# Two-layer expert network behind a channel attention: the first pair's v transposed on VectorE alone, with the opening rearranged around it

## The chip, the cores and the metric

The kernel runs on one core of one Trainium2 chip. The metric is the device time of one execution in microseconds (us); smaller is better. The engines are TensorE (PE for its matmuls, PEld for its weight loads), VectorE (DVE), ScalarE (ACT), GpSimd (POOL) and SyncE (SP), which here only issues DMAs.

## The reference

q, k and v are 6016 x 256, fp32. Channel attention, then two feed-forward layers:

```python
qn = q / (norm(q, axis=rows) + 1e-6); kn = k / (norm(k, axis=rows) + 1e-6)
s = kn.T @ qn / tau                    # 256 x 256
a = softmax(s, axis=-1)                # denominator + 1e-9
x = v @ a                              # 6016 x 256
h = x @ w_in;  x = (h * sigmoid(1.702 * h)) @ w_out        # 256 -> 2048 -> 256
h = x @ w2_in; out = maximum(0.01 * h, h) @ w2_out         # 256 -> 2048 -> 256
```

The weights come as 64-bit words and are turned into fp32 in the kernel.

## The kernel before, in words

**Numbers.** Most products are made of three fp32r matmuls over a high and a low half of each operand: (high, high), (low, high), (high, low), in the order that `terms` writes. `halves(hi, lo, raw)` makes the halves: a rounding copy on ScalarE gives the high half, and a subtraction on VectorE gives the low one.

**Stages.** First the kernel streams q and k and sums the 256 x 256 scores in two PSUM banks (y00 for half 0, y10 for half 1). The second half of the scores' last 16 rows is held back and handed to TensorE in portions, `second_half(count)`, so that it has work while the softmax is prepared. Instead of v @ a, the kernel folds a into the first layer's weights: `fold(f)` multiplies the softmax (halves `eth`, `etl`) with piece f of w_in (8 pieces, `wi`), scales it by the softmax's denominators (`fold_scale`) and makes the halves `wa[f]`. Piece 0 is folded in two halves by hand (kc = 0 after `softmax(0)`, kc = 1 after `softmax(1)`), as soon as each half of the softmax is there. Rows of v are handled in pairs of 512-column blocks (u = 0, 1), each in two halves of the channels (kc = 0, 1), with v turned so that channels lie on partitions: `xa[0]` holds kc = 0, `xbt` kc = 1. `first_products(kc, pairs)` are the first pair's products with piece 0, and `hidden_first(f)` is the rest of its hidden layer: activation (`act`), halves `gd`, later the products with w_out (`put`, `emit_y`).

**The first pair's v.** kc = 0 comes by eight DMAs of 64 KB each, in runs of 128 B (`blocks_in`/`blocks_of`: 32 x 32 blocks laid so that one VectorE transpose of 32 x 32 blocks, `turn_blocks(u)`, turns it). kc = 1 comes by one DMA of 512 KB in runs of 512 B, and TensorE turns it with eight 128 x 128 transposes (`transpose_v`) into the free PSUM banks y00 and y11. All of it lands in the place of the tenth q/k tile (`qk(V_TILE)`).

**The order.** Everything is written out by hand; each engine runs its instructions in the order of the program, and waits on semaphores. Weight pieces are turned into fp32 by a generator, `jobs()`, of which `go_on(n)` runs n steps. Each piece of w_in and w_out takes five steps on VectorE (`convert`): two or three integer operations (L211, L216, L220), then a copy for the high half and a subtraction for the low half. Numbering the steps from 1: wi0 is 1 to 5, wo0 6 to 10, wi1 11 to 15, wi2 16 to 20, wo1 21 to 25 (the subtraction is the last of each). Three pieces can be in flight. The third step of a piece frees its buffer, issues the next load (`next_load`) and calls `scale_next`, which has ScalarE scale the next landed piece (L181), unless `held` is set; `scale_next_piece` does so once by hand. `held` is set in the opening and cleared in `hidden_first(0)`:

```python
                    halves(gd[:, 0, u], gd[:, 1, u], h[:, u])
                    if f == 0 and u == 1:
                        held.clear()
                        scale_next()
                    go_on(1)
```

So the kernel before has run 12 steps when `hidden_first(0)` begins. In `hidden_first(0)` and `hidden_first(NF)` five more follow, then come `fold(1)`, which needs both halves of wi1 (step 15), two more, `hidden_first(1)` with `go_on(6)`, `fold(2)` and `go_on(2)`; the products of f = 1 with wo1 (step 25) follow.

Of the kernel before, what the change touches and what calls it, by code (L numbers as in the profile page):

```python
# [7 lines left out]
F32 = mybir.dt.float32  # L8
# [3 lines left out]
AF = mybir.ActivationFunctionType  # L12
# [5 lines left out]
def tile_kernel(  # L18
# [28 lines left out]
    nc = tc.nc  # L47
# [53 lines left out]
    def subtract(out, in0, in1):  # L101
        add(out, in0, in1, ALU.subtract)
# [11 lines left out]
    with tc.manual_schedule():  # L114
# [48 lines left out]
        def next_load():  # L163
            if to_load and len(raws) < 3:
                load_piece(to_load.pop(0))
# [21 lines left out]
        def scale_next_piece():  # L187
            held.clear()
            scale_next()
            held.append(True)  # L190
# [113 lines left out]
        def go_on(count):  # L304
            for _ in range(count):
                next(work, None)
# [25 lines left out]
        def qk(j):  # L332
            return big[(j // 2 + 2) % 4][:, j % 2]
# [18 lines left out]
        def blocks_of(x, p, u, kc, a):  # L352
            cols = slice(kc * P + a * SB, kc * P + (a + 1) * SB)
            s = start_of(p, u)
            return x[s:s + width[p], cols].rearrange("(b j) i -> j b i", j=SB)

        def blocks_in(t, p, a):
            return t[a * SB:(a + 1) * SB, :width[p]].rearrange("j (b i) -> j b i", i=SB)
# [57 lines left out]
        def second_half(count):  # L416
            for j, r in late_rows[:count]:
                scores(j, (1,), (r,))
            del late_rows[:count]
# [24 lines left out]
        for j in range(LATE + 1):  # L444
            t, n = qk(j), rows[j]
            scores(j, range(KC) if j < LATE else (0,))
            squares(j)
            if j + AHEAD <= last:
                load_qk(j + AHEAD)
            if j == V_TILE:  # L450
                next_load()
                nc.sync.dma_start(out=taub, in_=tau.partition_broadcast(P))
                vblocks = [qk(V_TILE)[:, 0, 2 * u:2 * u + 2, :].rearrange("p r c -> p (r c)") for u in range(2)]
                vrows = qk(V_TILE)[:, 1].rearrange("p r (s c) -> p (r s) c", c=P)
                for u in range(2):
                    for a in range(P // SB):
                        nc.sync.dma_start(
                            out=blocks_in(vblocks[u], 0, a), in_=blocks_of(v, 0, u, 0, a)
                        )
                nc.sync.dma_start(  # L460
                    out=vrows, in_=v[:2 * BLK, P:].rearrange("(t p) c -> p t c", p=P)
                )
                for _ in range(2):
                    next_load()

        for j in range(LATE + 1, last - 1):
            squares(j)
# [2 lines left out]
            scores(j, (0,))  # L470
        vt = {}

        def turn_blocks(u):
            vt[0, u] = front.tile([P, 2, C], F32, tag="sq", name="vt", bufs=6).rearrange("p r c -> p (r c)")
            nc.vector.transpose(out=vt[0, u], in_=vblocks[u])

        nc.vector.reciprocal(out=rtau, in_=taub)
        scale_next_piece()
        go_on(1)
        turn_blocks(0)  # L480
        second_half(1)
        norms()

# [14 lines left out]
        def spread():  # L498
            for kc in range(KC):
                nc.tensor.matmul(  # L500
                    nrm[:, C + kc * P:C + (kc + 1) * P],
                    lhsT=rn[:, kc:kc + 1].to_broadcast([P, P]), rhs=ident,
                    start=True, stop=True,
                )
            nc.scalar.copy(rq, nrm[:, C:2 * C])

        def transpose_v(tags):
            for u, tag in enumerate(tags):
                vt[1, u] = bank(tag)
                for i in range(BLK // P):  # L510
                    nc.tensor.transpose(  # L511
                        vt[1, u][:, i * P:(i + 1) * P], vrows[:, u * (BLK // P) + i], ident
                    )

        def split_v(kc, u):
            dst = xbt if kc else xa[0]
            halves(dst[:, 0, u], dst[:, 1, u], vt[kc, u])

        def softmax(h):

            nc.vector.tensor_tensor_reduce(
                out=sc[:, h], in0=s_ps[h][:, :C], in1=rq, scale=rk[:, h:h + 1],
                scalar=-3.0e38, op0=ALU.mult, op1=ALU.max, accum_out=mx[:, h:h + 1],
            )
            nc.vector.tensor_scalar(
                out=nmx[:, h:h + 1], in0=mx[:, h:h + 1], scalar1=-1.0, scalar2=None, op0=ALU.mult
            )
            nc.scalar.activation(
                out=ex[:, h], in_=sc[:, h], func=AF.Exp, bias=nmx[:, h:h + 1],
                scale=1.0, accum_out=den[:, h:h + 1],  # L530
            )

        def turn(h):
            for d in range(KC):
                nc.tensor.transpose(  # L535
                    et[:, h * C + d * P:h * C + (d + 1) * P], ex[:, h, d * P:(d + 1) * P], ident
                )

        def split_e(h):
            cols = slice(h * P, (h + 1) * P)  # L540
            src = et[:, h * C:(h + 1) * C].rearrange("p (d c) -> p d c", d=KC)
            nc.scalar.copy(eth[:, :, cols], src)
            subtract(etl[:, :, cols], src, eth[:, :, cols].bitcast(F32))
            nc.vector.tensor_scalar_add(rden[:, h:h + 1], den[:, h:h + 1], 1e-9)
            nc.vector.reciprocal(out=rden[:, h:h + 1], in_=rden[:, h:h + 1])
# [8 lines left out]
                    pw, lhsT=e[:, d, c0], rhs=wi[:, x, d], start=i == 0, stop=i == len(todo) - 1  # L554
                )

        def fold_scale(raw, pw, kc):
            nc.scalar.activation(
                out=raw[:, 0::3] if kc == 0 else raw[:, 1:3],
                in_=pw.rearrange("p (s n) -> p s n", s=2), func=AF.Copy,  # L560
                scale=rden[:, kc:kc + 1],
            )

        def fold_half(raw, f, kc):
            at = slice(0, 4, 3) if kc == 0 else slice(1, 3)
            hi, lo = wa[f][:, 0, at], wa[f][:, 1, at]
            (nc.vector.tensor_copy if kc else nc.scalar.copy)(hi, raw[:, at])
            subtract(lo, raw[:, at], hi.bitcast(F32))

        go_on(1)  # L570
        second_half(4)
        spread()
        nc.scalar.copy(xa[0][:, 0, 0], vt[0, 0])
        softmax(0)
        go_on(2)
        turn_blocks(1)
        go_on(1)
        second_half(5)
        et = bank("h3")
        turn(0)  # L580
        split_e(0)
        subtract(xa[0][:, 1, 0], vt[0, 0], xa[0][:, 0, 0].bitcast(F32))
        split_v(0, 1)
        scale_next_piece()
        go_on(1)
        second_half(2)
        wi0 = ready.pop(0)
        raw0 = early.tile([P, 4, P], F32, tag="tp", name="raw")
        pw = bank("y01")
        pw0 = [pw[:, kc * C:(kc + 1) * C] for kc in range(KC)]  # L590
        fold_products(pw0[0], wi0, 0)
        fold_scale(raw0, pw0[0], 0)
        fold_half(raw0, 0, 0)
        second_half(len(late_rows))
        transpose_v(("y00", "y11"))
        softmax(1)
        go_on(2)

        hp0 = {}

        def first_products(kc, pairs):
            for s, u in pairs:
                if kc == 0:
                    hp0[s, u] = bank(f"h{2 * s + u}")
                at = ((A11, A12), (A21, A22))[s][kc]
                x = xbt if kc else xa[0]
                terms(hp0[s, u], (wa[0][:, 0, at], wa[0][:, 1, at]), (x[:, 0, u], x[:, 1, u]),
                      kc == 0, kc == KC - 1)

        first_products(0, [(0, 0)])  # L610
        turn(1)
        split_e(1)
        scale_next_piece()
        go_on(1)
        split_v(1, 0)
        first_products(0, [(1, 0)])
        fold_products(pw0[1], wi0, 1)
        fold_scale(raw0, pw0[1], 1)
        fold_half(raw0, 0, 1)
        nc.sync.dma_start(out=w1raw[0], in_=raw0)  # L620
        split_v(1, 1)
        nc.scalar.preload_act_table(AF.Gelu_apprx_sigmoid)
        first_products(0, [(0, 1), (1, 1)])
        go_on(3)

        def fold(f):

# [412 lines left out]
```

## Time and profile before

| | |
|---|---|
| time, median of 3 runs | 1034.83 us (1034.72 to 1035.46) |
| the profiled execution's own time | 1034.38 us |
| its span, first to last instruction | 1032.6 us |
| TensorE matmuls busy | 1027.5 us (100%) |
| VectorE, ScalarE busy | 775.1 us (75%), 596.9 us (58%) |
| mean granted TensorE clock | 0.999 |

The span is what the trace covers; the execution's own time is 1.8 us longer. Matmuls are pipelined, and a matmul's recorded time includes the time in which it overlaps the next, so a row of n matmuls is best read by its start and the start of the row behind it. Times in the rows are us from the start of the span.

### The profile page before, as it was taken

The page shows a single profiled execution, that of the slowest core. Times are in us where ns is not written, and L with a number is a line of the kernel's source. Part 1 is how long each engine was busy: PE and PEld are TensorE (multiplying, and loading weights), DVE is VectorE, ACT ScalarE, POOL GpSimd, SP SyncE. Part 2 cuts the span into 40 slices and gives each one's busy share as a digit, 9 for nine tenths or more (in the row PEclk, how much of TensorE's full clock was granted, in tenths as well). Part 3 has the DMA queues.
Part 4 walks back from the last instruction along what each step waited for, and adds up shares of the span by engine and source line. Part 5 has one row for each costly group of instructions (what it writes and reads, how often), then busy time and mean ns, then how long its engine had stood idle before and what let it go on. Part 6 is the DMA issues. An engine that isn't in the chain of part 4 may idle for free.

```text
span 1032.6 us, 12743 instructions
## 1 busy us (share of the span) xinstructions
PE 1027.5 (100%) x4664; PEld 868.3 (84%) x4664; DVE 775.1 (75%) x1220; ACT 596.9 (58%) x906; POOL 0.8 (0%) x7
## 2 busy tenths in 40 slices
PE   9999999999999999999999999999999999999998
PEld 8888888888888888888998888888888888888997
DVE  7899868788888888887767666667577667667655
ACT  7675556566666666666555555555555555455453
POOL 0000000000000000000000000000000000000000
PEclk9999999999999999999999999999999999999999
DMA  9865323015115224214644003001100200300202
GB/s 352 249 163 153 126 49 92 11 31 165 60 52 168 77 65 126 80 56 150 239 150 144 1 1 72 11 1 31 52 0 16 67 1 1 77 1 1 42 1 36
DMA packets 124863, 81.84 MB, mean 79 GB/s; under 512 B 97664, under 2 KB 108928, under 8 KB 123520
## 3 DMA queue, kind: packets, MB, share of 16 engines
q1 hardware_dynamic: 120512, 80.04, 26.0%
q10 hardware_dynamic: 4288, 0.98, 0.5%
q8 instruction: 36, 0.59, 0.2%
q14 instruction: 27, 0.22, 0.1%
HBM read 55.05 MB, written 25.95 MB: 78 GB/s over the span
## 4 chain that ended last, share of the span: by engine, by line
PE 100%; DVE 0%; issue 0%
PE y L92 50%; PE h L92 44%; PE y L406 4%; PE h L553 1%; PE h L443 0%; PE y L553 0%; PE y L511 0%; PE h L426 0%; DVE o L706 0%; PE h L535 0%; PE h L500 0%
## 5 line engine op out<-in xcount | busy, mean ns | idle before, releaser
L92 PE MATMUL y<-gd,wo 128*128 128x512 f32 (+1 forms) x1248 | 296.2, 386 | 0.0
L92 PE MATMUL h<-xa,wa 128*128 128x512 f32 (+1 forms) x1152 | 276.1, 385 | 0.0
L92 PEld LDWEIGHTS y<-gd,wo 128*128 128x128 f32 x1248 | 233.9, 188 | 43.7
L92 PEld LDWEIGHTS h<-xa,wa 128*128 128x128 f32 x1152 | 216.0, 188 | 40.1
L92 PE MATMUL y<-g,wo 128*128 128x512 f32 (+1 forms) x1044 | 246.8, 385 | 0.0
L92 PEld LDWEIGHTS y<-g,wo 128*128 128x128 f32 x1044 | 196.0, 188 | 36.3
L92 PE MATMUL h<-xb,wa 128*128 128x512 f32 (+1 forms) x888 | 217.0, 385 | 0.0
L92 PEld LDWEIGHTS h<-xb,wa 128*128 128x128 f32 x888 | 166.6, 188 | 31.4 <-DVE wa L99 0.3
L99 DVE TENSOR_TENSOR tv<-tp,h 128x512 f32<-128x512 f32 (+1 forms) x88 | 59.2, 673 | 112.1 <-PE h L92 109.0
L99 DVE TENSOR_TENSOR cc<-tv,h 128x512 f32<-128x512 f32 (+1 forms) x176 | 115.8, 672 | 35.9 <-PE h L92 35.4
L96 DVE TENSOR_TENSOR gd<-cc,gd 128x1024 fp32r<-128x1024 f32 (+1 forms) x87 | 103.9, 1194 | 0.0
L877 ACT COPY tp<-h 128x512 f32<-128x512 f32 (+1 forms) x87 | 50.3, 578 | 91.3 <-PE h L92 90.7
L95 ACT CAST gd<-cc 128x1024 fp32r<-128x1024 f32 (+1 forms) x87 | 90.2, 1036 | 0.0
L650 ACT ACTIVATE cc<-cc 128x1024 f32<-128x1024 f32 (+2 forms) x49 | 50.3, 1027 | 39.1 <-DVE cc L99 39.1
L650 ACT ACTIVATE tt<-tt 128x512 f32<-128x512 f32 (+1 forms) x48 | 30.0, 625 | 72.3 <-DVE tt L99 72.3
L99 DVE TENSOR_TENSOR tt<-tv,h 128x512 f32<-128x512 f32 (+1 forms) x88 | 59.4, 675 | 9.6 <-PE h L92 0.5
L99 DVE TENSOR_TENSOR tt<-tt,h 128x512 f32<-128x512 f32 (+1 forms) x88 | 59.4, 675 | 9.5 <-DVE tt L99 0.5
L648 ACT ACTIVATE cc<-cc 128x1024 f32<-128x1024 f32 (+1 forms) x40 | 41.6, 1041 | 41.9 <-DVE cc L99 41.9
L99 DVE TENSOR_TENSOR g<-tt,g 128x512 fp32r<-128x512 f32 (+1 forms) x87 | 58.5, 673 | 7.2 <-ACT g L888 7.0
L648 ACT ACTIVATE tt<-tt 128x512 f32<-128x512 f32 (+1 forms) x40 | 24.9, 623 | 62.9 <-DVE tt L99 62.9
L99 DVE TENSOR_TENSOR g<-tp,g 128x512 fp32r<-128x512 f32 (+1 forms) x87 | 58.5, 673 | 0.1
L901 ACT CAST g<-tp 128x512 fp32r<-128x512 f32 (+1 forms) x87 | 53.2, 612 | 2.8
(110 smaller groups left out, 710.4 us busy)
## 6 DMA issues: line engine op xcount, KB each, us to landing
cv<-in_moe_w_in_dram SPq DMA_DIRECT2D x32, 256.0 KB, 3.4
cv<-in_moe_w_out_dram SPq DMA_DIRECT2D x16, 512.0 KB, 3.7
wa<-w2a SPq DMA_DIRECT2D x8, 896.0 KB, 5.6
x<-stg SPq DMA_DIRECT2D x5, 1024.0 KB, 4.2
stg<-x SPq DMA_DIRECT2D x5, 1024.0 KB, 5.2
out_dram<-o SPq DMA_DIRECT2D x80, 64.0 KB, 1.9
qk<-in_q_dram SPq DMA_DIRECT2D x8, 512.0 KB, 10.2
qk<-in_k_dram SPq DMA_DIRECT2D x8, 512.0 KB, 10.2
```

Of the source, the lines that this page charges most:

```text
L92: nc.tensor.matmul(dst, lhsT=w, rhs=x, start=start, stop=stop, skip_group_check=more)
L95: nc.scalar.copy(hi, raw)
L96: nc.vector.tensor_tensor(out=lo, in0=raw, in1=hi.bitcast(F32), op=ALU.subtract)
L99: nc.vector.tensor_tensor(out=out, in0=in0, in1=in1, op=op)
L406: nc.tensor.matmul(s_ps[h][:, :C], lhsT=t[:, 1, r, h * P:(h + 1) * P], rhs=t[:, 0, r, :], start=(j == 0 and r == 0), stop=(j == last and r ...
L553: nc.tensor.matmul(pw, lhsT=e[:, d, c0], rhs=wi[:, x, d], start=i == 0, stop=i == len(todo) - 1)
L648: nc.scalar.activation(out=out, in_=in_, func=AF.Gelu_apprx_sigmoid)
L650: nc.scalar.activation(out=out, in_=in_, func=AF.Prelu, alpha=0.01)
L877: nc.scalar.copy(tp, pa)
L901: nc.scalar.copy(g11[:, 0], tp)
```

## The change

The first pair's v is now loaded entirely as block loads: 16 DMAs of 64 KB instead of eight and one of 512 KB, with the weight pieces wo0 and wi1 issued after the second and the third group of four. VectorE turns all four blocks (`turn_blocks(kc, u)`), and TensorE's eight transposes go. The high and low halves of v are made by `v_high` (ScalarE) and `v_low` (VectorE) at places of their own. The second half of the softmax is rounded by VectorE instead of ScalarE. The second fold half's high part is written by ScalarE straight from PSUM, its low part is one VectorE operation from PSUM, and the raw half, which is only stored to DRAM, is written behind them. `first_products` takes the order (high, high), (low, high), (high, low) for kc = 0, and (high, high), (high, low), (low, high) for kc = 1. The load of ScalarE's Gelu table stands right behind the second Exp. The steps of `jobs()` are placed anew: 11 instead of 12 have run when `hidden_first(0)` begins, and step 8 stands behind the second fold half instead of in front of the first products.

```diff
-                vblocks = [qk(V_TILE)[:, 0, 2 * u:2 * u + 2, :].rearrange("p r c -> p (r c)") for u in range(2)]
-                vrows = qk(V_TILE)[:, 1].rearrange("p r (s c) -> p (r s) c", c=P)
-                for u in range(2):
+                vblocks = [
+                    qk(V_TILE)[:, i // 2, 2 * (i % 2):2 * (i % 2) + 2, :].rearrange("p r c -> p (r c)")
+                    for i in range(4)
+                ]
+                for i in range(4):
                     for a in range(P // SB):
                         nc.sync.dma_start(
-                            out=blocks_in(vblocks[u], 0, a), in_=blocks_of(v, 0, u, 0, a)
+                            out=blocks_in(vblocks[i], 0, a),
+                            in_=blocks_of(v, 0, i % 2, i // 2, a),
                         )
-                nc.sync.dma_start(
-                    out=vrows, in_=v[:2 * BLK, P:].rearrange("(t p) c -> p t c", p=P)
-                )
-                for _ in range(2):
-                    next_load()
+                    if i in (1, 2):
+                        next_load()
...
         scale_next_piece()
         go_on(1)
-        turn_blocks(0)
+        turn_blocks(0, 0)
+        go_on(1)
         second_half(1)
         norms()
...
-        def transpose_v(tags):
-            for u, tag in enumerate(tags):
-                vt[1, u] = bank(tag)
-                for i in range(BLK // P):
-                    nc.tensor.transpose(
-                        vt[1, u][:, i * P:(i + 1) * P], vrows[:, u * (BLK // P) + i], ident
-                    )
-
-        def split_v(kc, u):
+        def v_high(kc, u):
+            nc.scalar.copy((xbt if kc else xa[0])[:, 0, u], vt[kc, u])
+
+        def v_low(kc, u):
             dst = xbt if kc else xa[0]
-            halves(dst[:, 0, u], dst[:, 1, u], vt[kc, u])
+            subtract(dst[:, 1, u], vt[kc, u], dst[:, 0, u].bitcast(F32))
...
-            nc.scalar.copy(eth[:, :, cols], src)
+            (nc.vector.tensor_copy if h else nc.scalar.copy)(eth[:, :, cols], src)
...
-        def fold_half(raw, f, kc):
+        def fold_half(raw, f, pw, kc):
+
             at = slice(0, 4, 3) if kc == 0 else slice(1, 3)
             hi, lo = wa[f][:, 0, at], wa[f][:, 1, at]
-            (nc.vector.tensor_copy if kc else nc.scalar.copy)(hi, raw[:, at])
-            subtract(lo, raw[:, at], hi.bitcast(F32))
+            if kc == 0:
+                fold_scale(raw, pw, kc)
+                nc.scalar.copy(hi, raw[:, at])
+                subtract(lo, raw[:, at], hi.bitcast(F32))
+                return
+            fold_scale(wa[f][:, 0, :4], pw, kc)
+            nc.vector.scalar_tensor_tensor(
+                out=lo, in0=pw.rearrange("p (s n) -> p s n", s=2), scalar=rden[:, kc:kc + 1],
+                in1=hi.bitcast(F32), op0=ALU.mult, op1=ALU.subtract,
+            )
+            fold_scale(raw, pw, kc)
...
         go_on(1)
+        turn_blocks(0, 1)
         second_half(4)
         spread()
-        nc.scalar.copy(xa[0][:, 0, 0], vt[0, 0])
+        go_on(1)
         softmax(0)
-        go_on(2)
-        turn_blocks(1)
+        v_high(0, 0)
         go_on(1)
+        turn_blocks(1, 0)
+        v_low(0, 0)
         second_half(5)
         et = bank("h3")
         turn(0)
         split_e(0)
-        subtract(xa[0][:, 1, 0], vt[0, 0], xa[0][:, 0, 0].bitcast(F32))
-        split_v(0, 1)
+        v_high(0, 1)
+        v_low(0, 1)
         scale_next_piece()
         go_on(1)
+        turn_blocks(1, 1)
         second_half(2)
...
         fold_products(pw0[0], wi0, 0)
-        fold_scale(raw0, pw0[0], 0)
-        fold_half(raw0, 0, 0)
+        fold_half(raw0, 0, pw0[0], 0)
+        v_high(1, 0)
+        v_high(1, 1)
+        scale_next_piece()
         second_half(len(late_rows))
-        transpose_v(("y00", "y11"))
         softmax(1)
-        go_on(2)
...
-        first_products(0, [(0, 0)])
+        nc.scalar.preload_act_table(AF.Gelu_apprx_sigmoid)
+        v_low(1, 0)
+        go_on(1)
+        first_products(0, [(0, 0), (1, 0)])
         turn(1)
         split_e(1)
-        scale_next_piece()
-        go_on(1)
-        split_v(1, 0)
-        first_products(0, [(1, 0)])
+        v_low(1, 1)
+        first_products(0, [(0, 1)])
         fold_products(pw0[1], wi0, 1)
-        fold_scale(raw0, pw0[1], 1)
-        fold_half(raw0, 0, 1)
+        fold_half(raw0, 0, pw0[1], 1)
         nc.sync.dma_start(out=w1raw[0], in_=raw0)
-        split_v(1, 1)
-        nc.scalar.preload_act_table(AF.Gelu_apprx_sigmoid)
-        first_products(0, [(0, 1), (1, 1)])
-        go_on(3)
+        first_products(0, [(1, 1)])
+        go_on(4)
```

## Rows read from the trace of the kernel before

**Rows 1.** The page: busy us, share of the span and instructions of each engine

```profile
PE 1027.5 (100%) x4664; PEld 868.3 (84%) x4664; DVE 775.1 (75%) x1220; ACT 596.9 (58%) x906; POOL 0.8 (0%) x7
```

**Rows 2.** Timeline of TensorE's matmuls: start, us, instruction, out<-in, shape, count

```profile
48.28 1.04 PE L511 MATMUL y<-ident,qk 128*128 128x128 f32 x8
...
51.57 1.55 PE L92 MATMUL h<-xa,wa 128*128 128x512 f32 x6
52.96 3.04 PE L92 MATMUL h<-xb,wa 128*128 128x512 f32 x12
55.83 2.88 PE L92 MATMUL y<-gd,wo 128*128 128x512 f32 x12
58.55 0.64 PE L553 MATMUL h<-wi,eth 128*128 128x256 f32 x4
...
69.67 2.89 PE L92 MATMUL y<-gd,wo 128*128 128x512 f32 x12
```

**Rows 3.** Timeline of TensorE's weight loads; in brackets idle time and what ended it

```profile
49.85 0.20 PEld L535 LDWEIGHTS h<-ident,ex 128*128 128x128 f32 x2 [0.27 <-ACT ex L528]
```

**Rows 4.** Timeline of VectorE

```profile
47.86 0.42 DVE L99 TENSOR_TENSOR wa<-raw,wa 128x256 fp32r<-128x256 f32 x1
...
49.80 0.69 DVE L220 SCALAR_TENSOR_TENSOR ta<-cv,ta 128x512 int32<-128x512 int32 x1
...
57.58 0.69 DVE L99 TENSOR_TENSOR wi<-ta,wi 128x512 fp32r<-128x512 f32 x1
58.19 0.69 DVE L96 TENSOR_TENSOR gd<-h,gd 128x512 fp32r<-128x512 f32 x1
...
68.96 0.69 DVE L99 TENSOR_TENSOR wa<-raw,wa 128x512 fp32r<-128x512 f32 x1
```

**Rows 5.** Timeline of ScalarE

```profile
51.77 0.48 ACT L558 ACTIVATE raw<-y,rden 128x256 f32<-128x256 f32 x1
...
52.74 1.28 ACT L622 ACT_TABLE_LOAD   x1
...
56.92 0.57 ACT L648 ACTIVATE h<-h 128x512 f32<-128x512 f32 x1
57.53 0.62 ACT L95 CAST gd<-h 128x512 fp32r<-128x512 f32 x1
...
60.91 0.69 ACT L181 ACTIVATE cv<-cv 128x512 f32<-128x512 f32 x1
```

**Rows 6.** Timeline of SyncE: DMAs as they are issued

```profile
32.93 5.93 SPq L457 DMA_DIRECT2D qk<-in_v_dram  x8
...
39.44 0.58 SPq L157 DMA_DIRECT2D cv<-in_moe_w_out_dram  x1
...
50.56 0.37 SPq L157 DMA_DIRECT2D cv<-in_moe_w_out_dram  x1
...
61.45 2.09 SPq L725 DMA_DIRECT2D xr<-in_v_dram  x4
```

**Rows 7.** The page: DMA issues, count, KB each, median us to landing

```profile
cv<-in_moe_w_out_dram SPq DMA_DIRECT2D x16, 512.0 KB, 3.7
```

**Rows 8.** DMA issues of 61 to 82 us, columns as in the group above

```profile
xr<-in_v_dram SPq DMA_DIRECT2D x16, 64.0 KB, 2.6
```

**Rows 9.** VectorE's groups by shape, 28 to 140 us: busy us, mean ns | idle before

```profile
L475 DVE STREAM_TRANSPOSE vt<-qk 128x512 f32<-128x512 f32 x2 | 1.4, 708 | 0.0
...
L99 DVE TENSOR_TENSOR etl<-h,eth 128x256 fp32r<-128x256 f32 x2 | 0.8, 421 | 0.2 <-ACT eth L542 0.2
```

**Rows 10.** Busy time by stretch: engines (instructions), granted clock, DMA share, GB/s

```profile
4.00:6.00 2.00, 2.00 (x6) 1.55 (x6) 1.43 (x4) 1.26 (x5) 0.00 (x0) 1.00 0.91 272
...
37.00:38.00 1.00, 1.00 (x7) 0.87 (x6) 1.00 (x3) 0.00 (x0) 0.00 (x0) 1.00 0.64 94
...
41.00:42.00 1.00, 1.00 (x6) 0.87 (x6) 0.83 (x5) 1.00 (x1) 0.00 (x0) 1.00 1.05 312
...
1030.00:1033.00 3.00, 0.00 (x0) 0.00 (x0) 0.00 (x0) 0.00 (x0) 0.00 (x0) 0.56 0.43 70
```

More of the change, by code (lines that the diff above doesn't have):

```diff
@@ L471, in tile_kernel, with turn_blocks @@
         vt = {}
-        def turn_blocks(u):
-            vt[0, u] = front.tile([P, 2, C], F32, tag="sq", name="vt", bufs=6).rearrange("p r c -> p (r c)")
-            nc.vector.transpose(out=vt[0, u], in_=vblocks[u])
+        def turn_blocks(kc, u):
+            vt[kc, u] = front.tile([P, 2, C], F32, tag="sq", name="vt", bufs=6).rearrange("p r c -> p (r c)")
+            nc.vector.transpose(out=vt[kc, u], in_=vblocks[2 * kc + u])
         nc.vector.reciprocal(out=rtau, in_=taub)
@@ L555, in fold_products, with fold_scale @@
                 )
-        def fold_scale(raw, pw, kc):
+        def fold_scale(dst, pw, kc):
             nc.scalar.activation(
-                out=raw[:, 0::3] if kc == 0 else raw[:, 1:3],
+                out=dst[:, 0::3] if kc == 0 else dst[:, 1:3],
                 in_=pw.rearrange("p (s n) -> p s n", s=2), func=AF.Copy,
@@ L562, in fold_scale, with first_products @@
             )
-        def fold_half(raw, f, kc):
+        def fold_half(raw, f, pw, kc):
             at = slice(0, 4, 3) if kc == 0 else slice(1, 3)
             hi, lo = wa[f][:, 0, at], wa[f][:, 1, at]
-            (nc.vector.tensor_copy if kc else nc.scalar.copy)(hi, raw[:, at])
-            subtract(lo, raw[:, at], hi.bitcast(F32))
+            if kc == 0:
[9 more added lines that the diff above has]
+            fold_scale(raw, pw, kc)
+        def first_products(kc, pairs):
+            for s, u in pairs:
+                if kc == 0:
+                    hp0[s, u] = bank(f"h{2 * s + u}")
+                at = ((A11, A12), (A21, A22))[s][kc]
+                x = xbt if kc else xa[0]
+                wh, wl, ah, al = wa[0][:, 0, at], wa[0][:, 1, at], x[:, 0, u], x[:, 1, u]
+                order_of = ((wh, ah), (wh, al), (wl, ah)) if kc else ((wh, ah), (wl, ah), (wh, al))
+                for i, (w, a) in enumerate(order_of):
+                    nc.tensor.matmul(hp0[s, u], lhsT=w, rhs=a, start=kc == 0 and i == 0,
+                                     stop=kc == KC - 1 and i == 2)
+        hp0 = {}
         go_on(1)
+        turn_blocks(0, 1)
         second_half(4)
         spread()
-        nc.scalar.copy(xa[0][:, 0, 0], vt[0, 0])
+        go_on(1)
         softmax(0)
-        go_on(2)
-        turn_blocks(1)
+        v_high(0, 0)
         go_on(1)
+        turn_blocks(1, 0)
+        v_low(0, 0)
         second_half(5)
@@ L591, in tile_kernel @@
         fold_products(pw0[0], wi0, 0)
-        fold_scale(raw0, pw0[0], 0)
-        fold_half(raw0, 0, 0)
+        fold_half(raw0, 0, pw0[0], 0)
+        v_high(1, 0)
+        v_high(1, 1)
+        scale_next_piece()
         second_half(len(late_rows))
-        transpose_v(("y00", "y11"))
         softmax(1)
-        go_on(2)
[L599 to L608, printed above, removed]
-        first_products(0, [(0, 0)])
+        nc.scalar.preload_act_table(AF.Gelu_apprx_sigmoid)
+        v_low(1, 0)
+        go_on(1)
+        first_products(0, [(0, 0), (1, 0)])
         turn(1)
         split_e(1)
-        scale_next_piece()
-        go_on(1)
-        split_v(1, 0)
-        first_products(0, [(1, 0)])
+        v_low(1, 1)
+        first_products(0, [(0, 1)])
         fold_products(pw0[1], wi0, 1)
-        fold_scale(raw0, pw0[1], 1)
-        fold_half(raw0, 0, 1)
+        fold_half(raw0, 0, pw0[1], 1)
         nc.sync.dma_start(out=w1raw[0], in_=raw0)
-        split_v(1, 1)
-        nc.scalar.preload_act_table(AF.Gelu_apprx_sigmoid)
-        first_products(0, [(0, 1), (1, 1)])
-        go_on(3)
+        first_products(0, [(1, 1)])
+        go_on(4)
         def fold(f):
```

## The prediction, made blind

> **What bounds the kernel now.** I read the page first. TensorE's matmuls are busy 1027.5 us of a span of 1032.6, and no other engine is above 84% [rows 1]; the chain that ended last is TensorE's too. So a change counts only by the matmul time that it takes out and by the time for which it makes TensorE stand. Nothing behind the opening can give anything back, since TensorE has no idle time left there in which to catch up.
>
> Then the timeline of TensorE from 48 to 70 us. Read by starts, its matmuls of 512 columns follow each other every 0.23 us: six take 51.57 to 52.96, twelve 55.83 to 58.55 [rows 2]. In the opening the weight loads show small waits; the one that matters is 0.27 us for the second Exp, which frees `turn(1)` at 49.85 [rows 3]. All that the change can win lies there: the eight transposes (1.04 us in their row) and some tenths of waits, about 1.2 us in all. Measurement of this kernel tells about 0.2%, 2.07 us, from no change; a win of that size isn't in reach.
>
> Last, the timelines of VectorE, ScalarE and SyncE from 47 to 70 us, for what TensorE waits on next: VectorE has wi1's low half at 57.58 + 0.69 = 58.27 [rows 4], and TensorE first reads it with the third matmul of `fold(1)`, 58.55 + 2 x 0.12 = 58.78, where 0.12 is the pitch of a 256-column matmul (0.64 us for four with the overlap of the last) [rows 2]. That slack is 0.5 us.
>
> **The change part by part.**
>
> *The eight transposes go.* Without them TensorE runs the six matmuls of the first two products from 48.28 on, 6 x 0.23 = 1.4, to 49.66. `turn(1)` still waits for Exp until 49.85 [rows 3], so part of the gain turns into that wait. Behind `turn(1)` the order is as before with three matmuls fewer, so the products of xbt begin at 52.96 - 3 x 0.23 = 52.27: 0.69 us earlier.
>
> *Four VectorE turns instead of two, 2 x 0.71 us [rows 9].* The first extra one falls into time in which VectorE waits for the norms. The last one takes the place of a subtraction of nearly the same length, ahead of the first fold's low half, which so stays where it was: out at 47.86 + 0.42 = 48.28 [rows 4]. The second matmul, which now reads it, is due at 48.51. No cost, if the last block has landed when VectorE comes to it, 0.6 us (a turn's 0.71 less the overlap) before 47.86.
>
> *Sixteen block loads.* SyncE ends the first eight at 38.86. Then come wo0 (0.58), four blocks (2.09 for four in another stretch), wi1 (two issues like wo0, 1.2) and four blocks: 44.9 [rows 6]. The last issue begins near 44.4, and in that other stretch a block landed 2.6 us after its issue [rows 8]: 47.0, and VectorE comes to it at 47.26. While block loads moved, the DMA engines carried 94 GB/s at a busy share of 0.64; with longer runs it was 312 at 1.05 [rows 10]. By bandwidth, from 40.5 on (2.1 us behind the last of the first eight), wo0 and wi1 take 1.7 us each, and 256 KB of blocks 1.8 at the 147 GB/s of a full share: 47.5; 2.8 at 94 GB/s: 49.5. Bounds of the wait: nothing and 2.2 us. I take nothing, issue pace and landing of the same loads being the nearest rows.
>
> The Trainium skill, DMA: Bandwidth & Descriptors, "Why small descriptors are slow (HBM only)", says that each packet carries a fixed overhead, so that runs as short as these lose bandwidth. The trace agrees (94 against 312 GB/s); by the dearer of the two paces the last block comes 2.2 us late, and the forecast below would be 1039.2 instead of 1037.0.
>
> *Softmax rounding on VectorE.* At most 0.42 us, as a two-input operation of the same 256 columns from PSUM takes [rows 9]. It starts when `turn(1)` is through, near 50.35, and ends by 50.77; the fold that reads it comes at 50.83. No cost.
>
> *The second fold half from PSUM.* ScalarE's scaling can start at 51.77 as before, 0.48 us [rows 5], and now writes the high half itself: 52.25, where TensorE is ready for it at 52.27 (0.1 us to load the weights). The low half, one scalar-and-tensor operation of 256 columns from PSUM, isn't in the trace: between 0.42 [rows 9] and 0.69 (512 columns, L220 [rows 4]). I take 0.44, so 52.74. The third matmul wants it at 52.86. TensorE then ends the products of xbt at 55.20; before, it was 55.83. So far: -0.63 us.
>
> *The table load* (1.28 us [rows 5]) moves into ScalarE's idle time between 49.80 and 51.77. It costs nothing; in the old place it would now end at 54.02 again, and the first Gelu, which I expect at 53.3, would wait 0.7 us.
>
> *The steps of `jobs()`.* This is where I expect the loss. Before, step 8 ran at 49.80 and freed wo0's buffer, and SyncE issued wo1 at 50.56 [rows 4, 6]. Now step 8 stands behind the fold's low half: 52.74 + 0.61 = 53.35 (0.61 is VectorE's pitch, 57.58 to 58.19 [rows 4]). wo1 is issued at 53.42, and by the median of 3.7 us [rows 7] it lands at 57.15. And the count is one behind: step 13 was run before `held` was cleared in `hidden_first(0)`; now it comes after. Its `scale_next` therefore finds wi2 scaled and has ScalarE scale wo1 there, ahead of the third Gelu. Before, that scaling stood at 60.91, behind `fold(1)` [rows 5]. ScalarE would be free at 56.3 and waits for the landing until 57.2. Behind it queue: scaling 0.69, Gelu 0.57, rounding of gd 0.62 [rows 5]: 59.08. VectorE waits for that with gd's low half (0.69), and only then comes step 15, wi1's low half, since the count is one behind (before, it stood ahead of that gd: 57.58 and 58.19 [rows 4]): 59.12 + 0.61 + 0.69 = 60.41. TensorE ends its twelve y matmuls at 55.20 + 2.72 = 57.92, runs two matmuls of `fold(1)` and is due with the third at 58.15. It stands until 60.46: 2.31 us.
>
> *The step behind, once more.* Step 25, wo1's low half, ran in `hidden_first(1)` and now comes behind `fold(2)`'s last subtraction, which starts at 68.96 [rows 4]: in the old time scale it runs from 69.57 to 70.26. The second matmul of the row at 69.67 reads it, due at 69.90 [rows 2]; with the load of the weights it starts near 70.4. 0.5 us. Later pieces have slack, since each f runs 12 steps and needs 10.
>
> **Sum**, against the profiled execution's 1034.38 us: -0.63 + 2.31 + 0.5 = +2.18, so 1036.56. The median of the runs is 0.45 above that execution, so 1037.0 us: 0.21% slower. With the bounds of the single operations (0.25 for the low half, and estimates of 0.3 for wo1's landing and 0.3 for the last wait) this case spans 1036.3 to 1037.8.
>
> **The rivals.**
>
> *wo1 is there in time (not slower).* If it lands by 56.3, 2.9 us after its issue instead of 3.7, ScalarE doesn't wait, everything behind comes 0.95 us earlier, and the time is 1036.1, +0.12%. For it: TensorE and the DMA queue are otherwise quiet then. Against: the median over 16 such loads [rows 7]. It decides below 3.5 us, where the loss falls under 0.2%. If beside that VectorE's order hides step 15 altogether, only the -0.63 is left: 1034.2.
>
> *The last blocks come late.* Then the turn at 47.26, the fold's low half and the second softmax behind it slide, and step 8 with them: up to 2.2 us on the sum, 1037.2 to 1039.2, 1038 by the middle. It begins at a landing after 47.3, 0.3 later than I take it. For it: the bandwidth at 94 GB/s. Against: that stretch was not at full share.
>
> *The clock falls while TensorE stands.* With no matmul at the end of the kernel the mean granted clock of the last 3 us was 0.56 [rows 10]. In the first microseconds, where the clock column still prints 1.00, the pace was six matmuls in 2 us against seven in 1 us later, the low level of 1.2 GHz by its look [rows 10]. A stand of 2.3 us could bring that. Two to five us at half pace cost 1 to 2.5, less the 0.5 of the second wait, which VectorE would use to catch up: 1038.2. Against: no wait inside the kernel before has lowered it, but none was over 0.3 us.
> The Trainium skill, TensorE: Matmul & The Clock Gate, "HAM oscillation", has it that the clock goes back to half when TensorE idles between bursts; the end of this trace agrees, and no run here shows it for 2.3 us.
>
> *The change does what it says.* No new wait, 1.0 to 1.2 us won: 1033.7, still within 0.2%. Over 0.2% faster would need more matmul time than the change removes.
>
> **How the numbers follow.** The forecast 0.48, split at 1036.9 into 0.31 slower and 0.17 the same; wo1 in time or no wait 0.22, the same; late blocks 0.12 and the clock 0.15, slower; 0.03 for something that makes it faster by over 0.2%. So faster 0.03, same 0.39, slower 0.58. The range leaves out the cases with no new wait at all and the dearer part of late blocks and clock: 1034.6 to 1038.5 us.
>
> **What would show it.** The row of eight transposes is gone and products of xbt start near 52.3; a DMA wait on ScalarE at L181 near 57; TensorE standing some 2.3 us at the third matmul of `fold(1)`, released by VectorE's wi; a short wait at the y products behind `fold(2)`, released by wo. It is wrong if wi1's low half is out before 58.2, if the scaling of wo1 still stands behind `fold(1)`, or if VectorE waits for v's blocks near 47 us.

## The result, and the profile after

| | time, us | runs | TensorE's mean granted clock |
|---|---|---|---|
| before | 1034.78 (1033.90 to 1035.46) | 6 | 0.999 in the profile |
| after | 1040.96 (1038.98 to 1042.19) | 6 | 0.997 in four runs, 1.000 in two |

The ratio is 1.0059 [1.0046, 1.0072]: 6.2 us slower, outside the range of 1034.6 to 1038.5. The forecast had the sign and the largest of the new waits, and was 4 us short. The profiled execution took 1040.87 us, with a span of 1039.1; its clock was 0.997.

TensorE's timeline of the kernel after, around the opening (start, length, then engine, line, operation; in brackets the idle time before it and what ended it):

```profile
41.74 0.61 PE L501 MATMUL h<-ident,rn 128*128 128x128 f32 x4
...
50.32 1.41 PE L585 MATMUL h<-xa,wa 128*128 128x512 f32 x5 [1.60 <-DVE wa L99]
...
54.24 3.09 PE L585 MATMUL h<-xb,wa 128*128 128x512 f32 x12
57.16 2.88 PE L92 MATMUL y<-gd,wo 128*128 128x512 f32 x12
59.88 0.40 PE L549 MATMUL h<-wi,eth 128*128 128x256 f32 x2
62.62 0.51 PE L549 MATMUL h<-wi,eth 128*128 128x256 f32 x2 [2.34 <-DVE wi L99]
...
63.92 4.50 PE L92 MATMUL y<-gd,wo 128*128 128x512 f32 x12
...
75.84 2.83 PE L92 MATMUL y<-gd,wo 128*128 128x512 f32 x11 [0.26 <-DVE wo L99]
```

The row of eight transposes is gone. Against [rows 2] there are three new waits of over 0.2 us, at 50.32, 62.62 and 75.84. And at 63.92 twelve matmuls take 4.50 us, where the twelve at 57.16 take 2.72 by the next start (59.88).

The waits of TensorE's weight loads in the kernel after, 45 to 85 us (what waited and for what; us in total, times, longest):

```profile
PEld h L549 <- DVE wi L99: 2.5, 1, 2.5
PEld h L585 <- DVE wa L99: 2.0, 1, 2.0
PEld y L92 <- DVE wo L99: 0.7, 1, 0.7
...
```

VectorE's timeline of the same kernel:

```profile
44.58 0.71 DVE L475 STREAM_TRANSPOSE vt<-qk 128x512 f32<-128x512 f32 x1 [0.51 <-DMA qk<-in_v_dram]
...
49.24 0.71 DVE L475 STREAM_TRANSPOSE vt<-qk 128x512 f32<-128x512 f32 x1 [1.86 <-DMA qk<-in_v_dram]
49.88 0.38 DVE L99 TENSOR_TENSOR wa<-raw,wa 128x256 fp32r<-128x256 f32 x1
...
61.27 0.69 DVE L96 TENSOR_TENSOR gd<-h,gd 128x512 fp32r<-128x512 f32 x1 [1.57 <-ACT gd L95]
61.88 0.68 DVE L99 TENSOR_TENSOR wi<-ta,wi 128x512 fp32r<-128x512 f32 x1
```

ScalarE's:

```profile
57.65 0.69 ACT L181 ACTIVATE cv<-cv 128x512 f32<-128x512 f32 x1
59.44 0.66 ACT L181 ACTIVATE cv<-cv 128x512 f32<-128x512 f32 x1 [1.10 <-DMA cv<-in_moe_w_out_dram]
```

And SyncE's, its DMA issues (the last number is how many; wi1 is the two at 41.46, then the last four blocks, then wo1):

```profile
41.46 2.38 SPq L155 DMA_DIRECT2D cv<-in_moe_w_in_dram  x2
43.94 2.18 SPq L459 DMA_DIRECT2D qk<-in_v_dram  x4
...
55.69 0.39 SPq L157 DMA_DIRECT2D cv<-in_moe_w_out_dram  x1
```

VectorE comes to its last turn at 47.4 and finds the block not landed until 49.2; the first fold's low half stands behind that turn, and TensorE with it. Then wo1, issued at 55.69, lands just before 59.44; ScalarE has waited 1.10 us for it with the third Gelu behind, VectorE waits for that with `gd`'s low half, and wi1's low half comes out at 62.56.

The clock shows in the windows of the kernel after (window; busy time and count of PE, PEld, DVE, ACT, POOL; granted clock; DMA share, GB/s):

```profile
60.00:62.00 2.00, 0.28 (x3) 0.08 (x1) 0.73 (x2) 1.94 (x5) 0.00 (x0) 1.00 0.63 187
62.00:64.00 2.00, 1.38 (x11) 1.38 (x12) 1.50 (x3) 0.39 (x1) 0.00 (x0) 1.00 0.21 75
64.00:66.00 2.00, 2.00 (x7) 1.59 (x6) 0.98 (x2) 1.41 (x3) 0.00 (x0) 0.54 0.09 34
66.00:68.00 2.00, 2.00 (x7) 1.57 (x6) 1.90 (x5) 0.00 (x0) 0.00 (x0) 0.61 0.81 180
68.00:70.00 2.00, 2.00 (x10) 1.65 (x9) 1.93 (x4) 0.18 (x1) 0.00 (x0) 1.00 0.88 182
```

TensorE stood in two stretches, 48.7 to 50.3 and 60.3 to 62.6. Some 1.5 us after it had taken up work again the granted clock went to the lower of its two levels (1.2 of 2.4 GHz), and the two windows from 64 to 68 us print 0.54 and 0.61.

**Where 6.8 us of the profile went.** I match TensorE's matmuls of both traces and compare their starts. Ahead of the opening, where both kernels do the same, the trace of after is 0.37 us early (41.74 against 42.11 for the row of four transposes of `rn`; this offset varies from -0.4 to +0.9 among the profiles below and is part of no change). From there on:

| place | start before, after | lag | added |
|---|---|---|---|
| ahead of the opening | 42.11, 41.74 | -0.37 | |
| first y product | 55.83, 57.16 | 1.33 | 1.70 |
| third matmul of `fold(1)` | 58.78, 62.62 | 3.83 | 2.50 |
| end of the slow stretch | 62.05, 67.56 | 5.50 | 1.67 |
| second y matmul behind `fold(2)` | 69.89, 75.84 | 5.94 | 0.44 |
| last matmul | 1027.93, 1034.33 | 6.40 | 0.46 |

The forecast's sum was +2.18. The opening is 2.33 above its term (1.70 against -0.63) and the clock 1.67 (the sum had nothing for it); these two make 4.0 of the 4.6 that are missing.

### The profile page after: what moved, and what is told of

The parts are those of the page before. It is cut to its first block, busy times and chain, and to the rows that moved or that the text cites. A ratio compares the mean times of both kernels' runs of the same rounds, so it can differ in the third digit from the quotient of the medians.

```text
span 1039.1 us, 12738 instructions
## 1 busy us (share of the span) xinstructions
PE 1029.5 (99%) x4656; PEld 868.2 (84%) x4656; DVE 777.1 (75%) x1222; ACT 597.2 (57%) x906; POOL 0.8 (0%) x7
## 4 chain that ended last, share of the span: by engine, by line
PE 97%; DVE 1%; DMA 1%; ACT 0%; SPq 0%; issue 0%; DVEq 0%; ACTq 0%
PE y L92 49%; PE h L92 43%; PE y L406 4%; PE h L549 1%; DMA cv<-in_moe_w_out_dram 0%; DMA qk<-in_v_dram 0%; PE h L443 0%; PE h L585 0%; SPq L459 0%; DVE gd L99 0%; ACT h L657 0%; ACT gd L829 0%; PE y L549 0%; PE h L426 0%; DVE vt L475 0%
## 5 line engine op out<-in xcount | busy, mean ns | idle before, releaser
L92 PE MATMUL h<-xa,wa 128*128 128x512 f32 (+1 forms) x1140 | 272.8, 385 | 0.0
L92 PEld LDWEIGHTS h<-xa,wa 128*128 128x128 f32 x1140 | 213.8, 188 | 40.2 <-ACT raw L554 0.4
L92 PE MATMUL h<-xb,wa 128*128 128x512 f32 (+1 forms) x876 | 214.0, 385 | 0.0
L92 PEld LDWEIGHTS h<-xb,wa 128*128 128x128 f32 x876 | 164.4, 188 | 30.7
L886 ACT COPY tp<-h 128x512 f32<-128x512 f32 (+1 forms) x87 | 50.3, 578 | 90.8 <-PE h L92 90.2
L659 ACT ACTIVATE cc<-cc 128x1024 f32<-128x1024 f32 (+2 forms) x49 | 50.3, 1027 | 39.1 <-DVE cc L99 39.1
L99 DVE TENSOR_TENSOR tt<-tt,h 128x512 f32<-128x512 f32 (+1 forms) x88 | 59.4, 675 | 9.5 <-DVE tt L99 0.5
```

The source lines that it names most:

```text
L99: nc.vector.tensor_tensor(out=out, in0=in0, in1=in1, op=op)
L659: nc.scalar.activation(out=out, in_=in_, func=AF.Prelu, alpha=0.01)
L886: nc.scalar.copy(tp, pa)
```

## The experiments

The cause may lie in the order of the steps, in the blocks, in the clock, or in the rest of the rearrangement. Each of the first four runs takes one of these out. The times of before on the same chips are 1034.48, 1034.52 and 1034.54 us. "In the profile" is the lag of the last matmul less the offset ahead of the opening, as in the table above (after: 6.77). All edits but that of `e8_rest` are to the kernel after.

**e1_steps: the twelfth step is run before `hidden_first(0)` again, step 8 behind the second softmax.**

```diff
         split_e(1)
+        go_on(1)
```

> The changed kernel with one more step of jobs() (step 8 of wo0) run behind the second softmax's split, so that 12 steps have run when hidden_first(0) begins, as before the change. Theory A (three waits in a row, each from its own cause, and a fallen clock from the second): the blocks of v still come late (VectorE waits 1.9 us near 49), but the stand of 2.3 us at fold(1), the half clock behind it (1.4 to 1.7 us) and the wait for wo1's low half (0.44) are gone: about 4.4 us less than the changed kernel's 1041, so 1036.5, and the clock stays at 1.0 in every run. Rival B (the late block is the root, VectorE being late everywhere because of it): TensorE still stands over 1 us at fold(1), and the time is 1038 or more.

Measured: 1036.36 us, ratio 1.0020 [1.0011, 1.0029]; in the profile 1.62. The scaling of wo1 stands behind `fold(1)` again. The fold has no wait, and none is left at wo1. TensorE's timeline:

```profile
60.27 0.64 PE L549 MATMUL h<-wi,eth 128*128 128x256 f32 x4
```

VectorE's, at the last turn:

```profile
49.37 0.71 DVE L475 STREAM_TRANSPOSE vt<-qk 128x512 f32<-128x512 f32 x1 [2.03 <-DMA qk<-in_v_dram]
```

So one step makes 4.3 us of the 6.2 by the medians (6.18 - 1.88), and the blocks' wait is a separate one that stays. One thing came out otherwise than expected: the clock did not stay in every run. Two of the ten show a mean of 0.998 and took 1037.34 and 1037.81, where the other eight have a median of 1036.2. The only stand of over 0.6 us that the profile of e1 has there is the one at `wa`, 1.70 us.

**e2_other: the last turn reads a block that landed earlier.** A quarter of the first pair's v is a copy of another quarter; all loads and operations stay.

```diff
+        vblocks[3] = vblocks[2]
         turn_blocks(1, 1)
```

> The changed kernel with its last turn of v reading the third block instead of the fourth; the fourth is loaded all the same, but nobody waits for it (the products with that quarter of the first pair's v are made of the wrong quarter). Theory A: the 1.9 us wait of VectorE near 47 us goes and TensorE's 1.6 us wait at its second matmul with it; the stand at fold(1) stays at about 2.3 us and the clock still falls in most runs: about 1.9 us less, 1039. Rival B (the late block is the root): the stand at fold(1) goes too, and the time is 1036 or less.

Measured: 1039.13 us, 1.0044 [1.0031, 1.0057]. The wait at `wa` is gone (six matmuls unbroken in 1.73 us), the one in `fold(1)` stays, and four of five runs show a mean clock of 0.998. TensorE's timeline:

```profile
61.66 0.51 PE L549 MATMUL h<-wi,eth 128*128 128x256 f32 x2 [2.30 <-DVE wi L99]
```

The edit takes out the wait for the last block alone. The third group is late as well, here by more than in after (1.30 us against 0.51), and TensorE waits 1.0 us for what stands behind that turn. VectorE's timeline:

```profile
45.47 0.71 DVE L475 STREAM_TRANSPOSE vt<-qk 128x512 f32<-128x512 f32 x1 [1.30 <-DMA qk<-in_v_dram]
```

**e3_fill: TensorE is given work during its stand,** 20 extra matmuls of 256 columns into the bank that `fold(1)` then starts anew.

```diff
+            for _ in range(20 if f == 1 else 0):
+                nc.tensor.matmul(
+                    pw[:, 0], lhsT=eth[:, 0, :P], rhs=wi[:, 0, :C], start=True, stop=True
+                )
```

> The changed kernel with twenty extra matmuls of 256 columns (2.4 us) in front of fold(1), into the bank that fold(1) then overwrites, so that TensorE works through the time for which it stood. Nothing else moves. Theory A (the clock falls because TensorE stands there): the granted clock stays at 1.0 in every run, and the time is that of the changed kernel's runs without the fall, 1039 to 1040, 1.5 us less than those with it. Rival C (the fall has another cause, as the earlier waits near 49 us): the clock still falls in most runs, and the time is 1041 or a little more.

Measured: 1039.67 us, 1.0052 [1.0038, 1.0065]; the clock was 0.999 or more in all five runs. The stand is filled almost exactly, and the row of twelve y matmuls behind it is back at 2.74 us (64.08 to the next start at 66.82). TensorE's timeline:

```profile
59.81 2.56 PE L640 MATMUL h<-wi,eth 128*128 128x256 f32 x20
...
62.78 0.51 PE L549 MATMUL h<-wi,eth 128*128 128x256 f32 x2 [0.16 <-DVE wi L99]
...
64.08 2.91 PE L92 MATMUL y<-gd,wo 128*128 128x512 f32 x12
```

So the fall that after shows hangs on the stand at `fold(1)`: with it the clock fell in eight runs of eleven (after and e2), without it in none of eleven (here and in e4), although the earlier stand at `wa` (1.27 us in this profile) was still there. That an earlier stand never does it is not shown: in e1, where it is the only one (1.70 us), two runs of ten show a lower mean clock. By the medians over before (6.18 and 5.19) the fall is worth 1.0 us, in the profile 1.67, and between the four runs of after with it (1041.4 on average) and the two without (1038.98 and 1040.05) 1.9. So few runs don't tell these apart.

**e4_hold: only ScalarE's scaling of wo1 is put back behind `fold(1)`,** and the count of steps stays one behind. In `hidden_first(0)` wi2 is scaled by hand; `held` is cleared after the fold.

```diff
-                        held.clear()
-                        scale_next()
+                        scale_next_piece()
...
+                    held.clear()
+                    scale_next()
```

> The changed kernel with ScalarE's scaling of wo1 held back until fold(1) is written out, where it stood before; the steps stay as changed. Theory A: ScalarE's wait of 1.1 us for wo1's landing and the 0.6 us of the scaling itself leave the chain to wi1's low half, so that TensorE's stand at fold(1) shrinks from 2.3 to about 0.8 us, and the clock stays: 1038, some 3 us less. Rival D (the place of step 15 behind gd's subtraction makes the stand by itself): the stand stays at 2 us and the time at 1041.

Measured: 1037.62 us, 1.0031 [1.0019, 1.0042]. The stand shrinks to 0.64 us, the clock is 0.999 or more in all six runs, wo1's 0.7 us stays. TensorE's timeline:

```profile
61.76 0.51 PE L549 MATMUL h<-wi,eth 128*128 128x256 f32 x2 [0.64 <-DVE wi L99]
```

So of the 4.3 us that e1 gives back, 3.0 (6.18 - 3.14) hang on ScalarE's scaling of wo1 with its wait, and on the clock that falls through it; the remaining 1.3 fit VectorE's order: the rest of that stand (0.64), and wo1's low half.

**e5_steps_other: e1 and e2 together.** A quarter of the first pair's v is again a copy.

> Both edits at once: one more step of jobs() behind the second softmax's split, and the last turn of v reads the third block instead of the fourth (that quarter of the first pair's v is then wrong). Theory A: with both causes gone no wait over 0.6 us is left; the step-8 run alone lag was 1.4 us, of which the late block made 2.0, so the kernel is 0.3 to 0.6 us faster than before: 1034.0. Rival E (something else of the change costs time too): 1035.5 or more.

Measured: 1034.63 us, 1.0001 [0.9992, 1.0010], level with before. The two parts add up, in us over before by the medians:

| | last block late | last block there |
|---|---|---|
| step one behind | 6.2 (after) | 4.6 (e2) |
| step in place | 1.9 (e1) | 0.1 (e5) |

The step costs 4.3 and 4.5, the clock's fall included, the block 1.5 and 1.8. By the medians that is the whole loss. It also says that the transposes' time is not won even then: I had expected 1034.0. The next runs ask where it went. In the profile of e5, whose execution took 1035.51, VectorE still waits 0.88 us for the third group and TensorE 0.65 behind it, so a part of the blocks' lateness remains in some executions.

**e6_early_pool and e7_early: all sixteen blocks are issued in a row, wo0 and wi1 behind them;** the hand-called scaling and the steps move to suit (twelve run ahead of `hidden_first(0)`). In e6 GpSimd makes v's four low halves, in e7 VectorE as in after.

```diff
-                    if i in (1, 2):
-                        next_load()
+                for _ in range(2):
+                    next_load()
...
-            subtract(dst[:, 1, u], vt[kc, u], dst[:, 0, u].bitcast(F32))
+            nc.gpsimd.tensor_tensor(
+                out=dst[:, 1, u], in0=vt[kc, u], in1=dst[:, 0, u].bitcast(F32), op=ALU.subtract
+            )
```

(The second hunk is e6 alone.)

> The changed kernel with all sixteen block loads issued ahead of wo0 and wi1, the scalings and steps of these two moved behind the first fold half so that they come after their landing, 12 steps ahead of hidden_first(0), and the low halves of v made by GpSimd instead of VectorE. Theory A: the blocks land near 45 and 46, ahead of VectorE's turns; GpSimd takes 2.7 us off VectorE; no wait over 0.3 us is left: 1033.8 against 1034.5 before. Rival F (VectorE and GpSimd slow each other, or GpSimd takes over 2 us for one low half): the third matmul of the first products waits for it, and the time is 1035 or more.

> As the run with GpSimd, but the low halves of v stay on VectorE. Theory A: no wait for blocks; VectorE, which got 1.8 us more to do here than before, is late by some tenths at the second fold half and at gd: 1034.3 to 1035. Rival F (the load order alone is enough): as fast as the run with GpSimd, or faster if GpSimd is slow.

Measured: e6 1035.66 us, 1.0012 [1.0004, 1.0021]; e7 1034.97 us, 1.0004 [0.9995, 1.0012]. In e7 no turn waits for a block. SyncE's sixteen issues take 9.92 us, and the last six land 2.2 to 2.7 us after their issue. The last four of after took 3.5 to 4.5. The tile view of v's blocks in e7, issues from 41 to 45 us:

```profile
DMA to landing us min/median/max: 2.2/2.3/2.7
```

The same view of after, issues from 43 to 46.2 us (how many; ns of an issue, min/median/max; first and last start):

```profile
L459 SPq DMA_DIRECT2D qk<-in_v_dram x4: 473/510/544, 43.9 to 45.6; - x4
...
DMA to landing us min/median/max: 3.5/3.9/4.5
```

So the blocks are late because weight pieces stand ahead of them, and not by their own pace alone. In e6, which was to be the faster of the two (1033.8), VectorE is slowed while GpSimd works, as its rival F had it, though TensorE's wait comes at the second fold and not in the first products. GpSimd's timeline:

```profile
48.89 2.72 POOL L513 TENSOR_TENSOR xb<-vt,xb 128x512 fp32r<-128x512 f32 x2 [0.63 <-ACT xb L509]
```

VectorE's, at the same time:

```profile
49.72 0.76 DVE L211 TENSOR_SCALAR ta<-cv 128x512 int32<-128x512 int32 x1
50.58 1.58 DVE L216 SCALAR_TENSOR_TENSOR ta<-cv,ta 128x512 int32<-128x512 int32 x1
```

The same two operations in e7, which differs from e6 by GpSimd alone:

```profile
49.96 0.42 DVE L211 TENSOR_SCALAR ta<-cv 128x512 int32<-128x512 int32 x1
50.48 0.69 DVE L216 SCALAR_TENSOR_TENSOR ta<-cv,ta 128x512 int32<-128x512 int32 x1
```

`eth` comes late by it, and TensorE's weight load for the second fold waits 1.4 us.

**e8_rest: the rest of the change alone, on the kernel before.** v's rows, TensorE's transposes and the steps stay as before; VectorE rounds the second softmax, the second fold half comes from PSUM, and the table load stands behind the second Exp.

> The kernel before with the rest of the change alone: v's second half still in rows and turned by TensorE, all loads and steps as before; the second softmax rounded by VectorE, the second fold half from PSUM, the Gelu table behind the second Exp. Theory A: none of the three is on the chain that TensorE waits for: within 0.3 us of before, 1034.3 to 1034.8. Rival G (VectorE's longer rounding and the later low half cost time on their own): 0.5 us or more above before.

Measured: 1035.63 us, 1.0011 [1.0002, 1.0020]; in the profile 1.24. That is above the 1034.3 to 1034.8 expected; rival G came. So these edits cost about a microsecond where v's kc = 1 halves are still made in their old place. The trace shows two things, and no run parts them: ScalarE's table load, from 50.73 to 52.0, puts the fold's scaling back by 0.4 us (53.08, where 51.77 in before is 52.69 with the offset of 0.92), and the raw half, now written behind VectorE's low half, waits for that with v's last rounding behind it, which starts 1.65 us later than before. ScalarE's timeline:

```profile
54.34 0.47 ACT L558 ACTIVATE raw<-y,rden 128x256 f32<-128x256 f32 x1 [0.78 <-DVE wa L574]
54.71 0.58 ACT L95 CAST xb<-y 128x512 fp32r<-128x512 f32 x1
```

TensorE's waits for weights:

```profile
PEld h L92 <- ACT xb L95: 0.7, 1, 0.7
PEld h L92 <- DVE xb L96: 0.4, 1, 0.4
PEld h L92 <- DVE wa L574: 0.4, 1, 0.4
...
```

**e9_scalar: e7 with the second softmax rounded by ScalarE as before,** the table load behind that, and wi1's scaling between the fold's two scalings.

> The run with the blocks first and the low halves on VectorE, with the second softmax rounded by ScalarE again (the Gelu table behind that, the scaling of wi1 between the two scalings of the second fold half). Theory A (VectorE's time is what is left): the 0.7 us wait for eth and part of the 0.5 us for the low half go: 0.3 to 0.5 us less than that run, 1034.5, level with before and no faster. Rival H (ScalarE's table load, 1.28 us, now stands in the way of the second fold half): no gain or a loss, 1035 or more.

Measured: 1034.61 us, 1.0000 [0.9991, 1.0009]; in the profile -0.16. It is the best version that I found, and not faster than before. The waits of TensorE's weight loads in e9, 45 to 62 us:

```profile
PEld h L586 <- ACT wa L554: 0.5, 1, 0.5
PEld h L531 <- ACT ex L524: 0.5, 1, 0.5
PEld h L586 <- DVE wa L570: 0.3, 1, 0.3
PEld y L92 <- DVE gd L96: 0.2, 1, 0.2
PEld y L549 <- ACT eth L538: 0.2, 1, 0.2
```

Those of before over the same stretch:

```profile
PEld h L535 <- ACT ex L528: 0.3, 1, 0.3
PEld h L92 <- DVE wa L99: 0.3, 1, 0.3
PEld y L553 <- ACT eth L542: 0.2, 1, 0.2
```

They sum to 1.7 us against 0.8. In TensorE's starts, the transposes' going takes out 0.98 us (46.55 to 49.07 in before, 47.47 to 49.01 in e9), and of that 0.68 is given back by the first y product. So most of the transposes had stood in time in which TensorE would otherwise have waited for the second Exp and the second fold.

**e10_one_between: e1's step, and wi1 issued behind the last blocks, wo0 alone between.**

```diff
-                    if i in (1, 2):
+                    if i in (1, 3):
```

> The run with one more step, and wi1 issued behind the fourth group of blocks instead of the third, so that only wo0 stands among the blocks. Theory A (the fourth group is late because of wi1's 512 KB and the gaps around it): the last block lands 1.5 to 2 us earlier, near 47.3, VectorE's wait falls from 2.0 to under 0.5 us, and the time is 1034.8 to 1035.3 against 1036.4 with wi1 in front. Rival I (runs of 128 B are late by themselves, whatever stands between): the wait stays over 1 us and the time at 1036 or more.

Measured: 1035.82 us, 1.0011 [1.0002, 1.0020]: 0.6 us better than e1 by the medians (1.28 over before against 1.88; the two intervals overlap), but above the 1034.8 to 1035.3 that I expected. VectorE's last turn now waits 0.61 us instead of 2.03, but wi1 is late in its place, and ScalarE, which scales it ahead of the second Exp, waits. ScalarE's timeline:

```profile
50.01 0.68 ACT L181 ACTIVATE cv<-cv 128x512 f32<-128x512 f32 x1 [0.70 <-DMA cv<-in_moe_w_in_dram]
```

The weight load of `turn(1)`, which waits for that Exp:

```profile
51.22 0.20 PEld L531 LDWEIGHTS h<-ident,ex 128*128 128x128 f32 x2 [1.21 <-ACT ex L524]
```

The order of two loads on one queue only chose who waits; e7 and e9 moved the scaling as well.

## Why the prediction came out 4 us short

**The step that failed: "Sixteen block loads", bounds nothing and 2.2 us, of which I took nothing.** VectorE waited 1.86 us at the last block and 0.51 at the third group; a wait for v's blocks near 47 us was the last of the prediction's own signs of being wrong. By e1 and e5 the last block is worth 1.8 us. Of the 2.1 us between the landing that I worked out, 47.0, and the 49.1 that VectorE's start at 49.24 shows, 1.2 is issue: the last block was issued at 45.6 and not near 44.4, because wi1's two issues took 2.38 us. I had priced them like wo0's, 0.58 each [rows 6]. A nearer row stood in SyncE's timeline of before, and I passed over it:

```profile
40.06 5.64 SPq L155 DMA_DIRECT2D cv<-in_moe_w_in_dram  x4
```

Issues of the same loads, right behind the same kind of traffic, 1.41 us each. The other 0.9 is the landing, 3.5 us after the issue, the least of those four, instead of the 2.6 of [rows 8]. That 2.6 is a median over four groups of four blocks in unlike company: the two with no weight piece right ahead landed 2.1 to 2.7 us after issue, the one behind w_in's two loads 2.2 to 3.1, and the one issued at 64.11, right behind 512 KB of w_out, 3.0 to 3.7. The tile view of before for that group was the nearer row:

```profile
DMA to landing us min/median/max: 3.0/3.4/3.7
```

Both rows were of the same instructions but of another company. The bound by bandwidth, 2.2 us, was near the truth. The Trainium skill's rule on short runs (DMA: Bandwidth & Descriptors, "Why small descriptors are slow (HBM only)") pointed the same way. With the dearer of the two paces that the rows have, the forecast would have been 1039.2. e7 shows that short runs aren't the whole of it, since the same sixteen loads in a row kept pace with their issue and no turn waited.

**A second fault: cases that add up were priced as rivals.** Late blocks (0.12) and the clock (0.15) were each priced on top of the forecast's sum, but never together, and the forecast (0.48) stood without both. They lie in series, and all three came: opening 1.70 instead of -0.63, stand 2.50 for 2.31, clock 1.67 for nothing, wo1's low half 0.44 for 0.5. The forecast's own two waits came to 2.94 for 2.81. That is no luck: the late block put back TensorE's arrival at `fold(1)` (by 2.33 us at the first y product) and wo1's issue (by 2.27) alike, so the stand kept its size. The price of the clock, 1 to 2.5 us, holds 1.67, though the 2 to 5 us at half pace behind it came from no row of before; the profile of after has one stretch of 3.4, from 64.1 to 67.6. A stand of the forecast's own size lowered the clock in four runs of after's six and four of e2's five, so it belonged to the forecast.

**Point by point.** The transposes went, and `turn(1)` waits for Exp (0.4 us) as said. The softmax rounding took 0.42 us on VectorE, the fold's low half from PSUM 0.48 (0.44 taken). The table load is hidden in after, at 51.70 to 52.98; but in e8 it puts the fold's scaling back by 0.4 us, so this place isn't free by itself, and that it was hidden in after partly because everything else was late is only argued. wo1 landed 3.7 us after its issue as by [rows 7], 59.4 instead of 57.15 since it was issued 2.27 later; ScalarE's 1.10 us wait, VectorE's order behind it and the third matmul of `fold(1)` came as written; e4, which takes ScalarE's wait out, and e1, which takes the step out, bear that out. "wo1 is there in time" and "the change does what it says" are refuted. The claim that some 1.2 us can be won at most is not refuted, but the -0.63 as far as the first y product was not reached by any version: e9, without late blocks, gets -0.24 there (0.62 less its offset of 0.86), because the second Exp, the rounding behind it and the fold set the time, and not TensorE.

**Left open.** The last 0.46 us of the lag: 0.3 of it comes at 99 us, where a weight load waits 0.41 us for ScalarE's scaling of a later fold; it isn't in e1, but I made no run for it alone. And why the clock falls in some executions of one kernel and not in others: the two runs of e1 and the one of e6's eleven (1037.82) that show 0.998 left no trace that says after which stand it fell.

## What to carry to other kernels

Price a load by a row with the same neighbours on its queue, not by a row of the same load: here one half of a w_in piece took 0.63 us to issue in e7 (four from 44.65 in 2.52 us) and 1.41 in before, and a block landed 2.3 us after its issue in e7 and up to 4.5 in after. Write the waits that you foresee in the order of time and ask of each whether it excludes the next; those that follow each other on one path are summed, and a stand of TensorE such as the 2.3 us here gets the clock's fall on top. A helper that counts steps is part of the schedule: one `go_on(1)` fewer made two thirds of this loss.

## What the runs showed of the hardware

A stand of TensorE of 2.3 us amid steady work (2.34 in the profile of after, 2.30 in that of e2) was enough for the granted clock to fall to half, in eight runs of eleven. In the profile that cost 1.7 us. With the stand filled by dummy matmuls, or cut to 0.64 us, it fell in none of eleven. Where the longest stand in the profile was 1.70 us (e1), two of ten runs show a lower mean clock, 0.998.

GpSimd at work slows VectorE: while it made two low halves in 2.72 us, VectorE's integer operations took 0.76 us instead of 0.42 and, with two tensors as inputs, 1.58 instead of 0.69 (e6 against e7). The Trainium skill's GPSIMD Engine Reference, "Specifications", says that the two engines share their interfaces to SBUF and names VectorE's operations with two inputs there; the trace agrees for the second of the two, and shows that the first, with one tensor as input, was slowed as well.
